# An adaLN block with dilated local attention and a gated feed-forward on one core: softmax in PSUM, its results regrouped by DMA, norm statistics shared with ScalarE, and a new hand-written order

## Chip, cores, metric

One core of one Trainium2 chip. The metric is the device time of one execution in microseconds (us), as the median of several runs. Engines are called PE (TensorE), DVE (VectorE), ACT (ScalarE), POOL (GpSimd) and SP (SyncE, which here only issues DMAs).

## What is computed

```python
mod = (silu(c) @ w_mod).reshape(1, 6, 1, 512)       # sa, ca, ga, sb, cb, gb
h = layernorm(x) * (1 + ca) + sa
x = x + ga * A(h)
h = layernorm(x) * (1 + cb) + sb
x = x + gb * B(h)

# A: 32 heads of 16; a query looks at 8 keys, 2 positions apart, itself the last
q, k, v = heads(x @ wqkv)
idx = pos[:, None] - 2 * arange(8)[None, :]          # masked where idx < 0
attn = softmax(einsum('bhsd,bhswd->bhsw', q, k[idx]) * 16 ** -0.5)
o = einsum('bhsw,bhswd->bhsd', attn, v[idx]);  return o @ wo
# B:
return (gelu(x @ w_gate) * (x @ w_up)) @ w_down
```

2048 positions, model width 512, feed-forward width 1792, inputs and output in bf16.

## The kernel before

The 2048 positions are worked in four groups `sg` of 512 (four blocks `c4` of 128 positions). Each group passes through the same stages. Every stage is a small generator of operations `Op(engine, ...)`; the list `ORDER` at the top of the file names, one after the other, the generator whose next operation is issued. So the order of the instructions on every engine is written out by hand, stages of different groups are interleaved in it, and nothing reorders them later: an instruction that waits holds up all that stand behind it on its engine. The durations and latencies in the `Op` calls are notes for whoever wrote `ORDER`; they make no instruction. `tc.tile_pool` buffers are reused in turn, so a tile of a pool with n buffers waits for the readers of the tile n before it (`NB` holds the counts: four PSUM banks `mm` for matmul results, two `att`, one pair of banks `lg` for the logits).

The stages of a group, with the lines of the profile:

- LN1 (`norm`, L403): `bn_stats`/`bn_aggr` per block on DVE (L419, L420), `rstd` as a power on POOL (L429), normalised `xn` on DVE (L436). One norm, that of LN1 in group 3, is made by `norm_act` from ACT sums instead (L372, L382). `xn` is then transposed: by PE and identity (L451, L474) for the norms in `BY_PE` and for group 0, by a DMA transpose issued on SP (L457) for the others; ACT applies scale and shift (L489).
- q, k, v (L538, L556): 12 results of four 128x512 matmuls, cast to bf16 by ACT (L570, L572, L576). v is stored to DRAM (L582, `vscr`) and loaded back in four shifted copies, one for each 32 partitions (L591, tile `V4`, one buffer).
- Logits: DVE multiplies q by the 8 shifted k for each of four j (L611, `pq`, 128x4096 bf16), PE adds over partitions with a 0/1 matrix of 32 columns, in four column tiles (L625).
- Softmax over the window (`soft`, L633): maximum from PSUM (L642), difference into an SBUF tile `z` (L648), exponential on ACT in place (L653), sum (L658), reciprocal (L664), product `e` (L669). PE regroups `e` by 64 identity matmuls of 32 columns a group, 16 of them in line at a time (L680), and ACT casts the result to `PT` (L689).
- Values: DVE multiplies `PT` by `V4` (L700, `pv`), PE adds (L714), ACT casts (L725), PE applies `woP` (L735), DVE adds x (L744). `woP` was multiplied by the gate ga beforehand (L354).
- LN2, then the feed-forward: for each of 14 `ft`, g and u (L763, four 128x512 matmuls each), gelu and cast on ACT (L796, L803), product `hh` on DVE (L814; `gl` and `ub` have three buffers each); then y (L775, 14 matmuls for each `c4`; L786 for the last block), x added on DVE (L821, L828), store (L846, L837). `Wd` was multiplied by the gate gb (L349).
- The six vectors of `mod`: four as columns by 16 matmuls of one column each (L289), the two gates as full rows, broadcast over all partitions, by four 128x512 matmuls each (L303) and an ACT cast into `gB` (L308).

Matmuls with four column tiles (L625, L680, L714) run four at a time; below they are called quad blocks. The time of the exp and gelu tables is in rows `ACT_TABLE_LOAD` at L653 and L796; a silu table comes first, at L313.

## Time and profile before

| what | value |
|---|---|
| median of 3 runs | 248.04 us (247.26 to 250.15) |
| the profiled execution: its own time | 247.37 us |
| its span, first to last instruction | 245.5 us, so 1.9 us lie outside |
| busy: PE, DVE, ACT, POOL | 235.3, 180.0, 144.0, 16.6 us |
| granted TensorE clock | 1.000 |
| DMA traffic | 27.3 MB |

Columns of the page's groups: line, engine, operation, output<-inputs, shapes, count, then busy time and mean duration of one, then the idle time of the engine before them and what ended it. A matmul's duration counts its way through the array, so back-to-back matmuls overlap; the chain of waits, which gives each piece of work only the time until the next began, shows their real pitch.

### The profile page before, as it was taken

The page shows a single profiled execution, that of the slowest core. Times are in us where ns is not written, and L with a number is a line of the kernel's source. Part 1 is how long each engine was busy: PE and PEld are TensorE (multiplying, and loading weights), DVE is VectorE, ACT ScalarE, POOL GpSimd, SP SyncE. Part 2 cuts the span into 40 slices and gives each one's busy share as a digit, 9 for nine tenths or more (in the row PEclk, how much of TensorE's full clock was granted, in tenths as well). Part 3 has the DMA queues.
Part 4 walks back from the last instruction along what each step waited for, and adds up shares of the span by engine and source line. Part 5 has one row for each costly group of instructions (what it writes and reads, how often), then busy time and mean ns, then how long its engine had stood idle before and what let it go on. Part 6 is the DMA issues. An engine that isn't in the chain of part 4 may idle for free.

```text
span 245.5 us, 3731 instructions
## 1 busy us (share of the span) xinstructions
PE 235.3 (96%) x1431; PEld 110.9 (45%) x1445; DVE 180.0 (73%) x253; ACT 144.0 (59%) x252; POOL 16.6 (7%) x37
## 2 busy tenths in 40 slices
PE   7899678999999999999999999999999999999994
PEld 2655345544453444444444444444444444444444
DVE  4789899989999899898989898677824922222222
ACT  2379698883688576325765835268654424666400
POOL 3450011000400000010000001000000100000000
PEclk9999999999999999999999999999999999999999
DMA  6998699959916009209300592400000061000011
GB/s 168 379 382 269 124 201 250 415 189 217 202 46 208 0 7 211 45 16 201 108 1 3 105 223 44 128 23 0 3 0 0 0 131 64 1 0 3 0 43 43
DMA packets 29289, 27.32 MB, mean 111 GB/s; under 512 B 7256, under 2 KB 28120, under 8 KB 29272
## 3 DMA queue, kind: packets, MB, share of 16 engines
q1 hardware_dynamic: 28976, 26.83, 42.3%
q10 hardware_dynamic: 296, 0.26, 0.4%
q8 instruction: 11, 0.18, 0.3%
q14 instruction: 6, 0.05, 0.1%
HBM read 21.32 MB, written 4.19 MB: 104 GB/s over the span
## 4 chain that ended last, share of the span: by engine, by line
PE 79%; DVE 13%; DMA 4%; POOL 1%; issue 1%; POOLq 0%
PE u_ps L763 19%; PE g_ps L763 19%; PE y_ps L775 18%; PE qkv_ps L556 8%; PE x_ps L735 6%; DMA x<-in_A_x_dram 4%; DVE pq L611 4%; PE o_ps L714 3%; PE LTp L625 2%; DVE st L419 2%; DVE ssum L658 1%; POOL rstd L429 1%; PE y_ps L786 1%; DVE e L669 1%; DVE mx L642 1%; DVE z L648 1%
## 5 line engine op out<-in xcount | busy, mean ns | idle before, releaser
L763 PE MATMUL u_ps<-h,Wu 128*128 128x512 bf16 x224 | 57.5, 379 | 0.0
L763 PE MATMUL g_ps<-h,Wg 128*128 128x512 bf16 x224 | 57.5, 379 | 0.0
L796 ACT ACTIVATE gl<-g_ps 128x512 bf16<-128x512 f32 x56 | 33.6, 601 | 24.9 <-PE g_ps L763 20.6
L775 PE MATMUL y_ps<-Wd,hht 128*128 128x512 bf16 x203 | 45.9, 379 | 0.4
L803 ACT CAST ub<-u_ps 128x512 bf16<-128x512 f32 x56 | 33.0, 589 | 18.2 <-PE u_ps L763 18.1
L814 DVE TENSOR_TENSOR hht<-gl,ub 128x512 bf16<-128x512 bf16 x56 | 22.3, 419 | 29.1 <-ACT ub L803 29.0
L556 PE MATMUL qkv_ps<-hT,wqkv 128*128 128x512 bf16 x184 | 42.2, 380 | 0.0
L700 DVE TENSOR_TENSOR pv<-PT,V 128x4096 bf16<-128x4096 bf16 x16 | 35.8, 2286 | 2.1 <-ACT PT L689 2.1
L611 DVE TENSOR_TENSOR pq<-qT,kT 128x4096 bf16<-128x4096 bf16 x16 | 36.0, 2283 | 0.9 <-PE o_ps L714 0.7
L763 PEld LDWEIGHTS <-Wu 128*128 128x128 bf16 x224 | 21.4, 98 | 27.6 <-issue 2.5
L763 PEld LDWEIGHTS <-Wg 128*128 128x128 bf16 x224 | 21.6, 98 | 26.8 <-issue 1.3
L775 PEld LDWEIGHTS <-hht 128*128 128x128 bf16 x210 | 20.5, 98 | 25.0 <-issue 0.4
L556 PEld LDWEIGHTS <-wqkv 128*128 128x128 bf16 x184 | 20.2, 114 | 19.0 <-issue 2.3
L429 POOL TENSOR_TENSOR rstd<-rstd,neghalf 128x4 f32<-128x4 f32 (+1 forms) x8 | 11.7, 1462 | 174.0 <-DVE rstd L425 174.0
L821 DVE TENSOR_TENSOR ot<-y_ps,x 128x512 bf16<-128x512 f32 x15 | 10.3, 688 | 17.1 <-PE y_ps L775 13.6
L419 DVE BATCH_NORM_STATS2 st<-x 128x6 f32<-128x512 bf16 x28 | 18.9, 675 | 3.0 <-DMA x<-in_A_x_dram 2.9
L489 ACT ACTIVATE h<-h,modT,scl 128x512 bf16<-128x512 bf16 x12 | 8.8, 802 | 15.9 <-DMA h<-xn 15.9
L735 PE MATMUL x_ps<-woP,oT 128*128 128x512 bf16 x60 | 14.9, 379 | 0.2
L570 ACT CAST qT<-qkv_ps 128x512 bf16<-128x512 f32 x16 | 9.5, 601 | 6.5 <-PE qkv_ps L556 5.6
L744 DVE TENSOR_TENSOR x<-x_ps,x 128x512 bf16<-128x512 f32 x16 | 10.7, 684 | 2.7 <-PE x_ps L735 2.7
L572 ACT CAST kT<-qkv_ps 128x512 bf16<-128x512 f32 x16 | 9.5, 602 | 2.8 <-PE qkv_ps L556 2.8
L436 DVE TENSOR_SCALAR xn<-x,mv,rstd 128x512 bf16<-128x512 bf16 x28 | 9.8, 407 | 1.6 <-POOL rstd L429 1.6
(76 smaller groups left out, 175.8 us busy)
## 6 DMA issues: line engine op xcount, KB each, us to landing
V<-vscr SPq DMA_DIRECT2D x12, 520.0 KB, 9.2
wm<-in_w_mod_dram SPq DMA_DIRECT2D x6, 512.0 KB, 7.5
vscr<-vT SPq DMA_DIRECT2D x4, 512.0 KB, 3.8
out_dram<-ot SPq DMA_DIRECT2D x15, 128.0 KB, 1.7
Wg<-in_B_w_gate_dram SPq DMA_DIRECT2D x1, 1792.0 KB
Wu<-in_B_w_up_dram SPq DMA_DIRECT2D x1, 1792.0 KB, 12.8
wqkv<-in_A_wqkv_dram SPq DMA_DIRECT2D x3, 512.0 KB, 8.1
x<-in_A_x_dram SPq DMA_DIRECT2D x3, 512.0 KB, 8.0
```

The costliest lines, as they stand in the source:

```text
L419: nc.vector.bn_stats(out=st_k["st"][:, c4, :], in_=src()[:, c4, :])
L429: nc.gpsimd.tensor_tensor(out=st_k["rstd"][:, a:b], in0=st_k["rstd"][:, a:b], in1=neghalf[:, a:b], op=ALU.pow)
L556: nc.tensor.matmul(ps[:], lhsT=wqkv[blk][:, dt, j::4], rhs=B["hT", sg][:, :, dt, :], start=(dt == 0), stop=(dt == DT - 1))
L611: nc.vector.tensor_tensor(out=pq[:], in0=_ap(B["qT", sg][:, j, :], [[0, W], [1, SG]]), in1=_ap(kT[:, j, sg * SG + 2:sg * SG + 2 + SG], [[2 ...
L700: nc.vector.tensor_tensor(out=t[:], in0=_ap(B["PT", sg][:, 0, :], [[SG, 2], [0, 4], [1, SG]]), in1=_ap(v[:, 0, j, :], [[8, 2], [4 * (SG + ...
L735: nc.tensor.matmul(ps[:], lhsT=B["oT", sg][:, j, c4 * P:(c4 + 1) * P], rhs=woP[:, j, :], start=(j == 0), stop=(j == 3))
L744: nc.vector.tensor_tensor(out=x[:, c4, :], in0=B["x1ps", sg, c4][:], in1=x[:, c4, :], op=ALU.add)
L763: nc.tensor.matmul(ps[:], lhsT=Wt[:, dt, ft * P:(ft + 1) * P], rhs=B["h2T", sg][:, :, dt, :], start=(dt == 0), stop=(dt == DT - 1))
L775: nc.tensor.matmul(ps[:], lhsT=B["hh", sg, ft][:, c4 * P:(c4 + 1) * P], rhs=B["Wd", ft // 4][:, ft % 4, :], start=(ft == 0), stop=(ft == F ...
L796: nc.scalar.activation(out=gl[:], in_=B["g", sg, ft][:], func=ACT.Gelu_apprx_tanh)
L803: nc.scalar.copy(out=ub[:], in_=B["u", sg, ft][:])
L814: nc.vector.tensor_tensor(out=hh[:], in0=B["gl", sg, ft][:], in1=B["ub", sg, ft][:], op=ALU.mult)
```

## The change

- Softmax in place: the tile `z` is gone; the difference, the exponential and its sum work on the logits' PSUM tile `LTp`.
- Groups 1, 2 and 3 (`PT_DMA`): `e` is stored to DRAM and loaded back regrouped by four DMAs on SP, instead of 16 matmuls and two casts. Group 0 keeps PE.
- The gates: 16 matmuls of 32 columns by 128 in four column tiles give four rows of 128 values; ACT casts them, one DMA writes them to DRAM, another loads them broadcast into `gB`.
- Norm statistics: ACT makes them for 13 of the 32 blocks (before: 4), DVE for 19. `LN1.3` leaves `BY_PE`: its transpose is a DMA.
- The exp table is loaded ahead of the first softmax, by an exponential of four unused values.
- Head: x block 0 and 1 come by ACT's queue, 2 and 3 as one DMA by SP's; warm-up has 20 matmuls for 22; the load `wm4` stands behind `woP`; all `wm` share the two `h2` buffers. `prod` has 4 buffers for 3, `stat` 4 for 2. Logits and values use one j at a time in all groups.
- A new `ORDER` (and new notes of durations).

```diff
+PT_DMA = (1, 2, 3)
-          "wm": 1, ...  "prod": 3, "lt": 1, ...
+          ... "prod": 4, ...
+    gscr = {b: dram.tile([D], BF16, name=f"gscr{b}") for b in (2, 5)}
+    escr = {g: dram.tile([P, W, P], BF16, name=f"escr{g}") for g in PT_DMA}
...
-        def f():                                          # row(b, dst)
-            ps = T("mm", [P, D], F32, "mb_ps")
-            for kt in range(4):
-                nc.tensor.matmul(ps[:], lhsT=scB[:, kt, :], rhs=B["wm", b][:, kt, :], ...)
-        def g():
-            nc.scalar.copy(out=dst[:], in_=B["mb", b][:])
+    def gload(k):
+        def f0():
+            nc.sync.dma_start(out=gscr[b].rearrange("(c p) -> c p", p=P), in_=gR[0:P:H, k, :])
+        def f1():
+            nc.sync.dma_start(out=gB[:], in_=bass.AP(gscr[b].tensor, gscr[b].offset, [[0, P], [1, D]]))
+    def mods_g(k):
+            ps = T("mm", [P, P], F32, "gR_ps")
+            for kt in range(4):
+                for ch in range(4):
+                    nc.tensor.matmul(ps[H * ch:H * ch + H, :], lhsT=scB[:, kt, :],
+                                     rhs=B["wm", b][:, kt, ch * P:(ch + 1) * P], ..., tile_position=(0, H * ch))
+            nc.scalar.copy(out=gR[:, k, :], in_=B["mp", b][:])
...
+        yield Op("ACT", 0.15, lambda: nc.scalar.activation(out=junk[:], in_=neghalf[:], func=ACT.Exp), ...)
...
-    BY_ACT = ("LN1.3", )
+    ACT_CH = {"LN1.1": (3, 4), "LN1.2": (2, 4), "LN1.3": (0, 4), "LN2.0": (0, 2), "LN2.1": (0, 4)}
...
-    BY_PE = ("LN1.1", "LN1.2", "LN1.3", "LN2.0")
+    BY_PE = ("LN1.1", "LN1.2", "LN2.0")
...
-    GL = [[1, 1, 1, 1]] + [[2, 2]] * (NSG - 1)            # GV the same
+    GL = [[1, 1, 1, 1]] * NSG
...
-            B["z", sg] = T("lt", [P, W, P], F32, "z")
+            B["z", sg] = B["LT", sg]
...
+        if sg in PT_DMA:
+            return
+    def pt_dma(sg):
+        def f():
+            nc.sync.dma_start(out=escr[sg][:], in_=B["e", sg][:])
+        for a in range(4):
+            def f(a=a):
+                src = bass.AP(escr[sg].tensor, escr[sg].offset + a * P,
+                              [[W * P, H], [4 * P, 2], [H * W * P, CPS], [1, P]])
+                nc.sync.dma_start(out=B["PT", sg][H * (3 - a):H * (3 - a) + H, :, :]
+                                  .rearrange("p t (g s) -> p t g s", s=P), in_=src)
```

In the new `ORDER`, the work between the q, k, v of group 0 and the feed-forward stands so on DVE (counts behind the products; LN stands for the statistics and `rstd` of a norm, xn for its normalised blocks): LN1.1, xn1.1, pq.0 x4, LN1.2, mask, maximum and difference of group 0, xn1.2, pq.1 x1, sum, reciprocal, e.0, xn1.3, pq.1 x2, pv.0 x4, woP, pq.1 x1, x1.0, ..., e.1, pq.2 x4 with four hh, pv.1 x4. On PE the quad blocks of neighbouring j stand together in several places: 32 matmuls in a row for the logits of group 2 (with the gate gb's 16 behind them) and of group 3, and the last logits of group 1's third j next to the first values of group 0.

On SP: ..., vscr of group 0, its first two `V4` loads, the gate ga's store, the third `V4` load, vscr of group 1, the fourth `V4` load, the DMA transpose of LN1.3, the load of `gB`, `Wg`, `Wu`, vscr of group 2, group 1's `V4` loads, the store and four loads of group 1's softmax, `wm5`, ... For group 2 the five softmax DMAs stand behind the first two output stores; for group 3 the store stands before, and its loads behind, the last of group 3's four `V4` loads.

## The prediction

> **What bounds the kernel now.** I read the page first (busy times, the chain), then PE's timeline of the first 40 us, the chain in order of time, and the groups by shape.

> ```profile
> PE 235.3 (96%) x1431; PEld 110.9 (45%) x1445; DVE 180.0 (73%) x253; ACT 144.0 (59%) x252; POOL 16.6 (7%) x37
> ...
> PE 79%; DVE 13%; DMA 4%; POOL 1%; issue 1%; POOLq 0%
> ```

> PE bounds it; DVE's 13% must lie somewhere. PE's timeline (start, length, instructions; in brackets the wait before) shows where:

> ```profile
> 10.84 1.91 PE L538 MATMUL qkv_ps<-hT,wqkv 128*128 128x256 bf16 x16
> ...
> 25.05 0.61 PE L625 MATMUL LTp<-pq,Mph 128*32 128x512 bf16 x8 [0.56 <-DVE pq L611]
> 27.25 0.62 PE L625 MATMUL LTp<-pq,Mph 128*32 128x512 bf16 x8 [1.59 <-DVE pq L611]
> 27.80 5.37 PE L556 MATMUL qkv_ps<-hT,wqkv 128*128 128x512 bf16 x24
> 33.72 0.54 PE L289 MATMUL modT_ps<-scT,wm 128*128 128x1 bf16 x16 [0.55 <-ACT vT L576]
> 34.20 1.89 PE L556 MATMUL qkv_ps<-hT,wqkv 128*128 128x512 bf16 x8
> 37.46 0.62 PE L680 MATMUL PTp<-e,ident 128*32 128x256 bf16 x16 [1.37 <-DVE e L669]
> ```

> From 24 to 39 us PE waits for group 0's logits and softmax: 0.56 + 1.59 + 0.55 + 1.37 = 4.1 us. Later I find one wait, 0.44 us at 78.9, again for e (L669). Otherwise PE runs without a gap until 242.4; behind it lie 3.1 us of last addition and store. So the end moves by what PE no longer does, and by what it no longer waits. The chain in order of time (start, us until the next, what) prices PE's pieces:

> ```profile
> 125.15 0.55 PE PTp L680 x16
> 125.70 0.86 PE LTp L625 x16
> 126.56 0.97 PE u_ps L763 x4
> 127.53 0.86 PE g_ps L763 x4
> ...
> 131.85 0.98 PE o_ps L714 x16
> ```

> Four 128x512 matmuls take 0.86. A block of 16 quad matmuls takes 0.98 entering from full columns and 0.86 behind another quad block, and the first full group after it 0.97: 0.86 of work and 0.22 for the two switches. Eight take 0.43 of work (0.55 with the entry), and a group of 16 PTp also 0.43.

> **PE's work after the head** (against the profiled span).
> - PTp of groups 1 to 3 is gone: 3 x 0.43 = -1.3. ACT loses six casts of 0.5.
> - LN1.3's transposes (16 at L451, 0.89 in the chain): -0.9.
> - Gate gb: four 128x512 (0.86) become 16 quads of 128 columns, four in line: by the pitch of 0.86 / 4 for 512 columns, 4 x 0.054 = 0.2, behind a quad block without a switch: -0.6. (ga lies in the head, where PE waits anyway before; -0.4 there.)
> - Switches: behind group 0's PTp there are 17 separate quad blocks before and 11 after, although single j are used everywhere, because the new order puts them side by side: 6 x 0.22 = -1.3.

> Sum -4.1, and -0.4 for the wait at 78.9.

> **The head.** DVE starts the chain when x of group 1 lands (11.56 before; the same 2.6 MB come first, so I take 11.3). Three blocks of statistics at 0.82 (one is ACT's) end at 13.8; POOL 1.4 from DVE's add to DVE's xn (106.05 to 107.45 in DVE's timeline): 15.25; four xn 1.3: 16.6; four products at 2.22 end at 25.4, where before they end at 27.2. There POOL's rstd took 3.17 us at 15.21 because a product ran beside it; now DVE waits for POOL and that does not occur, since only short or PSUM-fed work follows the power each time. PE's second logits block thus begins at 25.4 and 12 q, k, v results of group 1 follow (10.4), with LN1.2's transposes (0.9) in between: 37.9. The eight logits matmuls of group 1's first j end at 38.4; e is due at 25.4 + LN1.2's two blocks 1.8 + mask 0.3 + 1.26 + 1.14 + xn 1.3 + pq 2.2 + sum + 0.98 + 1.14 = 35.5 + sum.

> ```profile
> L658 DVE TENSOR_REDUCE ssum<-z 128x128 f32<-128x1024 f32 x4 | 7.6, 1910 | 0.0
> ...
> L642 DVE TENSOR_REDUCE mx<-LTp 128x128 f32<-128x1024 f32 x4 | 4.9, 1222 | 0.9 <-PE LTp L625 0.9
> ```

> These groups by shape (busy us, mean ns, idle) show one reduction of one shape: 1.91 from SBUF, 1.22 from PSUM. Reading PSUM now, the sum costs 1.22 to 1.91; I take 1.25, its new source's row. e is ready at 36.8 (37.4 at worst), before PE needs it at 38.4. PTp ends at 39.0, 0.9 later than before (38.1), but with four more results of group 1 (3.5), LN1.2's transposes (0.9) and the first logits block (0.5) behind it: a lead of 4.0 us. The start of q, k, v, at 10.84 before, may come 0.4 earlier (DVE's wait of 0.38 for x's last block, which now travels in SP's first DMA); that is counted in the 4.0.

> [...]

> Nothing else in the head is free by itself. ACT's statistics of group 1 (0.63 + 0.12 + 0.72) stand before its first cast and wait for x: 11.3 to 12.8; then scB (a quarter of L359's elements, 0.62 for all: 0.3) and the casts at 0.49. The first q is cast at 13.6 to 13.7, and PE needs its bank at 13.9; if x lands 1 us later, PE loses 0.8. The exp table (1.28) fills ACT's idle 1.86 before scl (L297); it takes 1.28 off ACT's path to e.0, which other DVE work covers now. wm4 waits for the ga matmuls (20.3) and lands about 24.5, under the wait for logits. The third `V4` load is behind ga's store, the fourth behind group 1's v (35.2), landing about 41.3 (5.5 as its shortest row); group 0's values start at 43 (36.8 + xn 1.3 + two products 4.4 = 42.5 and slack). LN1.3's DMA transpose is issued at 38.3 to 38.9 and lands 4.2 later; ACT comes to its four scalings at 44.3. Behind it `Wg` and `Wu` are issued at 41.5 to 43 instead of 37 to 39 and need 12.8: 56, against a first g at 68.

> **Group by group.** I followed the engines' order with these pitches. PE: values of group 0 at 47.9 and 52.3 (waits 0.3), x1 at 53.8 to 58.0 (0.3), LN2.0 transposes at 64.1, g0 at 68.4, y of group 0 at 100.8 (before 105.9, then with 16 logits matmuls of group 2 still to do, 1.1), y of group 1 at 144.8. Waits that I find, for a bank, a `gl` buffer or oT: 0.3 + 0.3 + 0.3 + 0.1 + 0.2 + 0.1 = 1.3 us. ACT's 12 us more of statistics (9 blocks of 0.63 + 0.72) fall beside x1 and the waiting of ACT for PE (20.6 and 18.1 in the waits).

> The DMA route of the softmax is the unmeasured part. The DMA rows (count, KB, us from issue to landing):

> ```profile
> V<-vscr SPq DMA_DIRECT2D x12, 520.0 KB, 9.2
> ...
> vscr<-vT SPq DMA_DIRECT2D x4, 512.0 KB, 3.8
> out_dram<-ot SPq DMA_DIRECT2D x15, 128.0 KB, 1.7
> ```

> The 256 KB store lies between the last two: 2.4. Then four issues at 0.6 and the last load's landing. No row has 64 KB in pieces of 256 bytes; low 1.7, as the 128 KB store, high 9.2, as the `V4` loads. I take 2.3, since `V4`'s rows carry eight times the bytes and queue behind each other. From e to PT: 0.1 + 2.4 + 0.1 + 1.8 + 2.3 = 6.7 us, bounds 6.1 and 13.6 (PE and ACT before: e ends at 78.8, values start at 80.4, 1.6). Covered by: group 1, four products and four hh, 10.2; group 2, one product, two ot, maximum, difference and two hh with their wait for g and u, 7.7; group 3, `hh`, x, statistics, xn, 8.3. PE's next quad block then has 2, 1.5 and 2.1 us of slack. Nothing to pay at 6.7.

> **Sum.** -4.0 - 4.1 - 0.4 + 1.3 = -7.2: span 238.3, run 240.2 against 247.37. The median lies 0.67 above the profiled run, so 240.9; I say 241.0. Own range 239 to 243: without any of the 1.3, 239.6, and 0.5 below that if x lands early; with 2 us of waits that I overlooked, 243.

> **Rivals.**
> 1. Half the gain: the head's lead is lost. If x of group 1 or its casts come 1.5 us late, PE loses most of that, and LN1.3's transpose or the fourth `V4` load, late by 2.5 (the spread of the `V4` landings is 5.5 to 13.4), holds ACT and DVE: -7.2 + 1.2 + 2.0 = -3.2, 244.8. For it: 0.2 us between cast and bank; against: these loads have no neighbours.
> 2. No change to speak of: hh in feed-forward 0 starves. DVE does nine products and `Wd`'s scaling (7 x 0.6) there, with `gl` three deep; each product displaced by a late one costs 2.2, three of them 6.6: 247.4 on the median's scale. For it: ACT's waits for hh, 4.1 us before. Against: DVE has 10 us less to do overall (9 blocks of 0.82, four sums of 0.66).
> 3. Slower: the round trip of the softmax. Each us beyond 6.7 is covered by 5.5, 2.5 and 3.7 us in groups 1, 2, 3, and then stops DVE's values, hence x1 and LN2, and PE. At the high bound, 13.6, it costs 1.4 + 4.4 + 3.2 = 9.0: 250.0. It decides from about 13.0, where it eats 7.2. For it: the `V4` rows, whose tail is 13.4; against: eight times the bytes. [...]
> 4. The change does not do what it says, the sum staying at 1.91 from PSUM and the quad blocks switching between every j (10 more switches, 2.2): -4.5, 243.5.

> **Numbers.** Forecast 0.64; rival 1 0.12, 2 0.06, 3 0.10, 4 0.08. A measurement of this kernel tells about 1% (2.5 us) from no change. Faster by over 1% (below 245.6): forecast, rival 4 and most of 1, 0.82; same: rival 2 and the rest of 1, 0.08; slower 0.10. The range goes to 246.0, with rivals 2 and 3 beyond, and down to 239.0.

> **What would show it.** Right: PTp of group 0 near 39 with group 1's q, k, v behind it and no wait over 1.5 us before; sum rows at 1.25; no PE wait in the 50 us of feed-forward 0 above 0.5; PT landing under 7 us after e; PE's end near 235.2. Wrong: DVE pv waiting for a DMA (rival 3); ACT waiting for hht by more than 6 us (2); DVE or ACT waiting for x, V or hT by DMA before 50 us (1); 0.97 behind every eight quads (4).

## The result, and the profile after

The changed kernel takes 241.27 us (median of 4 runs, 240.55 to 242.38) against 248.59 for the kernel before beside it: a ratio of 0.971 (95% interval 0.964 to 0.978), 7.3 us less. Run once more in the experiments it gave 0.972 (0.966 to 0.977); there the medians are 5.6 us apart (246.65 and 241.04), since the kernel before, 248.59 in the first set, has medians of 246.65 to 247.26 in the four later ones. Forecast were 241.0 us and a span of 238.3; the profiled execution took 241.38 us, with a span of 239.6 (before 247.37 and 245.5). So the median fits better than the working: of 7.2 us predicted on the profiled span, 5.9 came. Medians and ratios leave disturbed executions out, among them the profiled ones of the repeat (405.95 us) and of the longer softmax route (249.63 us), whose profile serves only to show which waits occur.

The page of the changed kernel, busy times and the chain's shares:

```profile
PE 232.5 (97%) x1392; PEld 109.6 (46%) x1403; DVE 170.0 (71%) x238; ACT 150.7 (63%) x287; POOL 12.4 (5%) x37
...
PE 90%; DMA 4%; ACT 4%; issue 0%; ACTq 0%; DVE 0%
```

DVE's 13% of the chain are gone, but 4% of ACT are new. DMA had 4% before, for x; of its 4% now half is the load of `wm`. PE's timeline of the head shows where:

```profile
10.87 1.91 PE L543 MATMUL qkv_ps<-hT,wqkv 128*128 128x256 bf16 x16
...
22.97 0.55 PE L292 MATMUL modT_ps<-scT,wm 128*128 128x1 bf16 x16 [0.20 <-ACT kT L577]
23.45 1.05 PE L630 MATMUL LTp<-pq,Mph 128*32 128x512 bf16 x16
26.04 0.55 PE L292 MATMUL modT_ps<-scT,wm 128*128 128x1 bf16 x16 [1.55 <-DMA wm<-in_w_mod_dram]
26.52 1.55 PE L630 MATMUL LTp<-pq,Mph 128*32 128x512 bf16 x16
28.00 8.22 PE L561 MATMUL qkv_ps<-hT,wqkv 128*128 128x512 bf16 x32
...
40.50 0.62 PE L630 MATMUL LTp<-pq,Mph 128*32 128x512 bf16 x8
40.95 0.64 PE L688 MATMUL PTp<-e,ident 128*32 128x256 bf16 x16
```

The waits for products, a cast and e, 4.1 us before, are gone. In their place stands one of 1.55 us for the load of `wm4`. Behind it work is longer than its kind: the second 16 logits matmuls take 1.55 where the first took 1.05. The windows (stretch; length, busy time of PE, PEld, DVE, ACT, POOL; granted clock; DMA share; GB/s) say why:

```profile
26.00:27.00 1.00, 0.96 (x25) 0.70 (x29) 0.94 (x3) 1.00 (x6) 0.00 (x0) 0.96 0.11 35
27.00:28.00 1.00, 1.00 (x12) 0.16 (x5) 0.42 (x3) 0.94 (x5) 0.45 (x1) 0.50 0.09 16
...
30.00:31.00 1.00, 1.00 (x5) 0.48 (x4) 1.00 (x2) 1.00 (x2) 0.00 (x0) 0.83 1.14 253
```

The granted clock is 0.50 for some 3.4 us, from the end of the 27th us to the 31st, and 1.00 everywhere else; that takes half of it from PE, some 1.7 us (an estimate; the experiments measure it). In the profile of before it was 1.00 throughout.

One mark divides the rest: the start of the first feed-forward matmul. It is 73.8 us before and 70.4 after (predicted 68.4); from there to the end of the span it is 171.7 before and 169.2 after. The head gave 3.4 us, the work behind it 2.5.

Three views answer to those shown of before. The chain in order of time:

```profile
78.37 1.84 PE LTp L630 x32
80.21 0.22 PE gR_ps L345 x16
80.44 0.97 PE u_ps L786 x4
```

Thirty-two logits matmuls and the gate's sixteen stand behind one entry and one exit, as priced (0.2 for the gate). The groups by shape, and the DMA rows of 60 to 160 us (count, KB, us to landing):

```profile
L647 DVE TENSOR_REDUCE mx<-LTp 128x128 f32<-128x1024 f32 x4 | 4.9, 1221 | 0.1
L663 DVE TENSOR_REDUCE ssum<-LTp 128x128 f32<-128x1024 f32 x4 | 4.8, 1212 | 0.0
```

```profile
escr<-e SPq DMA_DIRECT2D x3, 256.0 KB, 2.5
PT<-escr SPq DMA_DIRECT2D x12, 64.0 KB, 2.4
```

The sum takes 1.21 us from PSUM (1.91 from SBUF before). The 64 KB loads in pieces of 256 bytes land in 2.4 us.

### The profile page after: what moved, and what is told of

It reads as the page before. It is cut to its first block, busy times and chain, and to the rows that moved or that the text cites. A ratio compares the mean times of both kernels' runs of the same rounds, so it can differ in the third digit from the quotient of the medians.

```text
span 239.6 us, 3678 instructions
## 1 busy us (share of the span) xinstructions
PE 232.5 (97%) x1392; PEld 109.6 (46%) x1403; DVE 170.0 (71%) x238; ACT 150.7 (63%) x287; POOL 12.4 (5%) x37
## 4 chain that ended last, share of the span: by engine, by line
PE 90%; DMA 4%; ACT 4%; issue 0%; ACTq 0%; DVE 0%
PE g_ps L786 20%; PE u_ps L786 20%; PE y_ps L798 19%; PE qkv_ps L561 14%; PE x_ps L758 6%; PE o_ps L737 3%; PE LTp L630 3%; DMA wm<-in_w_mod_dram 2%; DMA c<-in_c_dram 2%; PE y_ps L809 1%; ACT hT L494 1%; ACT gl L395 1%; PE warm_ps L210 1%; PE qkv_ps L543 1%; ACT vT L581 1%; PE modT_ps L292 1%
## 5 line engine op out<-in xcount | busy, mean ns | idle before, releaser
L798 PEld LDWEIGHTS <-hht 128*128 128x128 bf16 x210 | 20.6, 98 | 24.8
L561 PEld LDWEIGHTS <-wqkv 128*128 128x128 bf16 x184 | 20.6, 114 | 20.3 <-issue 3.5
L443 POOL TENSOR_TENSOR rstd<-rstd,neghalf 128x4 f32<-128x4 f32 (+1 forms) x9 | 8.6, 956 | 160.2 <-DVE rstd L437 89.6
L406 DVE BATCH_NORM_STATS2 st<-x 128x6 f32<-128x512 bf16 x19 | 12.8, 675 | 2.9 <-DMA x<-in_A_x_dram 2.9
L748 ACT CAST oT<-o_ps 128x512 bf16<-128x512 f32 x16 | 8.8, 592 | 5.5 <-PE o_ps L737 5.4
L581 ACT CAST vT<-qkv_ps 128x512 bf16<-128x512 f32 x16 | 9.2, 605 | 1.2 <-PE qkv_ps L561 1.2
## 6 DMA issues: line engine op xcount, KB each, us to landing
wm<-in_w_mod_dram SPq DMA_DIRECT2D x6, 512.0 KB, 5.8
vscr<-vT SPq DMA_DIRECT2D x4, 512.0 KB, 3.7
out_dram<-ot SPq DMA_DIRECT2D x15, 128.0 KB, 1.7
wqkv<-in_A_wqkv_dram SPq DMA_DIRECT2D x3, 512.0 KB, 9.3
x<-in_A_x_dram SPq DMA_DIRECT2D x3, 512.0 KB, 8.6
```

The costliest lines, as they stand in the source:

```text
L406: nc.vector.bn_stats(out=st[:], in_=src()[:, c4, :])
L561: nc.tensor.matmul(ps[:], lhsT=wqkv[blk][:, dt, j::4], rhs=B["hT", sg][:, :, dt, :], start=(dt == 0), stop=(dt == DT - 1))
L581: nc.scalar.copy(out=B["vT", sg][:, j, :], in_=ps[:])
L798: nc.tensor.matmul(ps[:], lhsT=B["hh", sg, ft][:, c4 * P:(c4 + 1) * P], rhs=B["Wd", ft // 4][:, ft % 4, :], start=(ft == 0), stop=(ft == F ...
```

## The experiments

**The head.** The theory: the wait for `wm4` and the clock behind it ate what the head was to give. `wm4` stands behind the four `woP` loads in SP's queue, and takes an `h2` buffer that gate a's matmuls must free first (issued at 20.93). The rival: casts and statistics on ACT, over which the chain runs from 32 to 41 us, hold the head. The kernel again, to see how steady its clock is:

> The kernel after once more, unchanged, beside the other three on the same chip, to have a second profiled execution of it and a tighter ratio. Expected: 0.97 times the kernel before. If a pause of PE of about 1.5 us is near the point from which the granted clock falls, the load of wm4 lands between 25.0 and 26.3 us (as it did in the kernels that share it), PE waits for it 1.0 to 1.8 us, and the clock behind it is 0.50 in some executions and 1.00 in others; if the fall has another cause, it is at 27 us again.

241.0 us, ratio 0.972. Its profile can't be read for the landing of `wm4`, but its executions answer the question on the clock: with those of the first result there are nine, whose median of 241.15 is meant by "after" below. Eight had a mean granted clock of 0.985 to 0.993 and took 240.55 to 242.38; the ninth had 0.999 and took 239.38. So the fall comes in most executions, not in all, and costs about 1.8 us by the one without it. The kernel before knows it too: of 17 executions beside `a_wm4_wo` below, four had 0.993 (248.95 to 249.43), thirteen 0.998 or more (246.07 to 247.19).

`wm4` in another buffer, same place in the queue:

```diff
-                B["wm", b] = T("h2", ...)
+                B["wm", b] = T("q" if b == 4 else "h2", ...)
-            yield Op("SP", 0.6, ldwm(4), take=[SL["h2"]], ...)
+            yield Op("SP", 0.6, ldwm(4), take=[SL["q"]], ...)
```

> The kernel after, with the load of wm4 taking its buffer from the pool of the later q tiles instead of the h2 tiles, so that it no longer waits until gate a's matmuls have read one. In the kernel after, this load is issued at 20.93 and PE waits 1.55 us for it at 26.04; behind that wait the granted clock is 0.50 for about 3.3 us. Theory (the wait sets back the head, and the pause behind it costs the clock): the wait goes, 1.2 to 1.6 us, and if the halved clock goes with it another 1.0 to 1.7; the time falls by 1.2 to 2.7 us against the kernel after, to 238.6 to 240.1. Rival (the stretch from 28 to 41 us is bound by the ACT engine's casts and statistics, which end no earlier): the time falls by at most 0.5 us. Between them: the wait goes and the clock still falls, because the little transposes of the gates are what lets it fall: 1.0 to 1.5 us.

241.2 us, ratio 0.975 (0.972 to 0.978): nothing gained. The load was issued at 17.16 in place of 20.93 and landed at 25.92 all the same, behind the `woP` loads (three of them landed at 23.7 to 24.7); PE waited 1.82 and the clock fell to 0.50. The buffer alone was not the cause.

The wait filled, with the load where it was:

```diff
+            if b == 4:
+                wp = T("mm", [P, SG], F32, "fill_ps")
+                for _ in range(7):
+                    nc.tensor.matmul(wp[:], lhsT=gB[:, 0:P], rhs=gB[:], start=True, stop=True)
```

> The kernel after, with seven more 128x512 matmuls of zeros, whose result nobody reads, ahead of the second modulation's matmuls for wm4, so that PE works through the wait at 26.04 instead of standing. Theory (a pause of PE lets the granted clock fall to 0.50): the load lands when it did, so the 1.55 us of wait stay (filled), the clock stays at 0.95 or above from 27 to 31 us, and the time falls by 1.0 to 1.7 us against the kernel after. Rival one (the clock's fall has another cause, say the sparse transposes and modulations around it): the clock still falls and the time is 0 to 0.5 us longer. Rival two (ACT bounds the stretch behind): the clock stays up and the time falls by at most 0.5 us.

239.82 us (238.69 to 240.52), ratio 0.970 (0.967 to 0.973). All six executions had a clock of 1.000; the first feed-forward matmul started at 69.1 (70.4), and 169.2 us followed as before. PE does 1.5 us more of useless work and the kernel is 1.3 us shorter than after by the medians: the clock's fall was the pause's doing, and its price is 1.3 by this run (1.8 by the one execution above). ACT alone does not bound that stretch.

`wm4` ahead in the queue, first too far (ahead of `x3`, `wm2`, `wm3` and `woP`; `x3` behind `wm3`):

```diff
             yield Op("SP", 0.55, ldx(2), ...)
-            yield Op("SP", 0.55, ldx(3), ...)
+            yield Op("SP", 0.6, ldwm(4), take=[SL["q"]], ...)
             ...                                   # wm2, wm3
+            yield Op("SP", 0.55, ldx(3), ...)
             ...                                   # woP, without wm4 behind it
```

> The kernel after, with the load of wm4 put ahead of the loads of wm2, wm3, x3 and wo in SyncE's queue (buffer from the pool of the later q tiles; x3 behind wm3). In the variant that only took the other buffer, the load was issued at 17.16 in place of 20.93 and landed at 25.92 all the same: the DMA engines were 99 per cent busy until 22 us, and the four wo loads ahead of it took 9 us each. Theory (wm4 is late because of what stands ahead of it in the queue): it lands before 21, PE's wait at 24 to 26 us is gone or under 0.3, the clock stays at 1.00, and the time falls by 1.3 to 2.6 us against the kernel after (ratio to before 0.960 to 0.966). Rival (ACT and DVE, not PE, set the head's end; or wm2, wm3 or x3, now one block later, are waited for instead): at most 0.5 us.

242.2 us, ratio 0.978 (0.973 to 0.983): 1.1 longer than after by the medians, against the theory's 1.3 to 2.6 shorter. The chain tells what came in its place:

```profile
13.83 10.37 DMA x<-in_A_x_dram
24.20 0.02 issue
24.22 0.72 ACT gl L384 x2
24.94 0.48 ACT kT L577
25.43 0.02 issue
25.45 2.31 DVE pq L616
```

`x3` was issued late and landed at 24.20. ACT's statistics of it stand in ACT's queue ahead of a cast of k, the last product needs that cast, and PE waited 2.3 us for the product, the clock falling to 0.50 again: the rival's case. `wm4` was in time. Then moved ahead of `woP` alone, where the kernel before has it (and with its buffer from the other pool, as above):

```diff
+            yield Op("SP", 0.6, ldwm(4), take=[SL["q"]], ...)
             for i in range(4):
                 yield Op("SP", 0.45, ld(woP[H * i:H * i + H, :, :], wo_v[i]), ...)
-            yield Op("SP", 0.6, ldwm(4), take=[SL["h2"]], ...)
```

> The kernel after, with the load of wm4 ahead of the four wo loads in SyncE's queue, where the kernel before has it, and its buffer from the pool of the later q tiles; nothing else in the queue moves. Theory (wm4 is late because it stands behind the wo loads; in the variant that put it ahead of x3 too, x3 came late, ACT's statistics of x3 stood before a cast of k, and PE waited 2.3 us for the product instead): wm4 lands at 22 to 24, PE does not wait for it, x3 is where it was, and the clock stays at 1.00; the first feed-forward matmul starts 1.2 to 2.5 us earlier than the 70.4 of the kernel after, and the time is 238.5 to 240.0 (ratio 0.960 to 0.967). Rival (some other operand of that stretch, x2, x3 or the products, then ends 1 us later and PE waits as long): within 0.5 us of the kernel after.

238.25 us (238.12 to 239.09), ratio 0.964 (0.959 to 0.969). Its slowest run is below the fastest of the nine of after, and its clock was 1.000 in all six. This version beats both kernels. Place and buffer were changed together; the place alone was not tried. Its PE timeline:

```profile
22.63 1.05 PE L630 MATMUL LTp<-pq,Mph 128*32 128x512 bf16 x16
24.04 0.55 PE L292 MATMUL modT_ps<-scT,wm 128*128 128x1 bf16 x16 [0.36 <-DMA wm<-in_w_mod_dram]
24.52 1.23 PE L630 MATMUL LTp<-pq,Mph 128*32 128x512 bf16 x16
25.68 7.10 PE L561 MATMUL qkv_ps<-hT,wqkv 128*128 128x512 bf16 x32
...
37.50 0.72 PE L688 MATMUL PTp<-e,ident 128*32 128x256 bf16 x16
```

The eight q, k, v results take 7.10 where they took 8.22, and group 0's turn comes at 37.5, not 40.95. The first feed-forward matmul starts at 67.2, 1.2 earlier than predicted, and again 169.2 us follow. Of the 3.2 us against after, 0.4 come from an earlier start of q, k, v in this profile (10.43 against 10.87).

**The softmax by DMA.** The turns of groups 1 to 3 (16 matmuls a group by the traces, 64 in all four and not in each) given back to PE and ACT, with `ORDER` otherwise kept. Three placings were tried, since `ORDER` was written for the DMA.

```diff
-PT_DMA = (1, 2, 3)
+PT_DMA = ()
 ORDER = [   # a group's five entries of pt_dma out, three of soft in (turn, cast, cast)
```

> The kernel after, with the softmax results of groups 1 to 3 turned by PE transposes with two ACT casts each again, in place of five DMAs each. Theory (PE's queue is the path, each turn costs it about 0.65 us): the time rises by 1.9 us (1.3 to 2.4) against the kernel after. Rival (the DMA round trip of 7 to 8 us from e to the turned tile is what PE's sums with v wait for, and the turn by PE takes 1.6 us): the time stays within 0.5 us or falls.

250.64 us, ratio 1.013 (1.009 to 1.017): 9.5 longer than after. The waits (sum, times, longest):

```profile
ACT PT L696 <- PE PTp L687: 8.1, 3, 4.5
...
PE g_ps L785 <- ACT gl L818: 2.9, 1, 2.9
```

The casts stood in ACT's queue ahead of the GELUs that free PE's banks: ACT stood, then PE, then the clock fell to 0.50, twice for 3.4 us. That tells of the placing.

> The kernel after, with the softmax results of groups 1 to 3 turned by PE and two ACT casts again, and each turn set behind feed-forward matmuls whose results ACT has already queued ahead of its casts. In the first variant of this kind the casts stood in ACT's queue ahead of the GELUs that empty PSUM: ACT waited 4.5 us for the turn and PE 2.9 us for ACT, the clock fell twice, and the time was 9 us longer, which tells of that placing and not of the turn. Theory (a turn costs PE 0.6 to 0.7 us and nothing else): 1.9 us longer than the kernel after (1.3 to 2.5). Rival one (the DMA round trip of 7 to 8 us costs as much as it saves): within 0.5 us. Rival two (ACT's two casts, 1.1 us, delay the GELUs that PE waits for, wherever the turn stands): 3 us longer or more, with PE waits on ACT behind each turn.

246.4 us, ratio 0.996 (0.991 to 1.000): 5.3 longer than after. Group 2's turn now came at 125.7, its values were late, and PE waited 2.2 us for them and 0.7 for x.

> The kernel after, with the softmax results of groups 1 to 3 turned by PE and two ACT casts each, third placing: group 1's turn 2.6 us earlier and group 2's 4.3 us earlier than in the second, each behind two GELUs that ACT has queued ahead of its casts. In the second placing the sum closed as: three turns of 0.7, 2.1; waits of PE for group 1's and group 2's products with v and for x, 2.9; a halved clock behind the longest of them, 1.6. Theory (those waits came from the placing, the turn itself costs 0.7): 1.9 to 2.6 us longer than the kernel after, with no PE wait above 0.5 us after 70 us. Rival (ACT's two casts delay the GELUs wherever the turn stands, or DVE's products come late in any case): 4 us longer or more, with PE waits on ACT or on products.

245.64 us, ratio 0.994 (0.990 to 0.997): 4.5 longer than after. The theory's 1.9 to 2.6 did not come, the rival's 4 did. From the first feed-forward matmul to the end it takes 174.2 us, 5.0 more than after. PE is busy 2.7 longer (235.2 against 232.5); its waits there add up to 2.4. Two of 0.48 are for ACT's cast `ub`, right behind the turns; the largest, 1.22, is for group 2's values. DVE's timeline shows for group 1 how a turn delays them:

```profile
77.51 0.43 DVE L834 TENSOR_TENSOR hht<-gl,ub 128x512 bf16<-128x512 bf16 x1 [2.12 <-ACT ub L823]
...
80.72 6.69 DVE L720 TENSOR_TENSOR pv<-PT,V 128x4096 bf16<-128x4096 bf16 x3
```

`PT` of group 1 was ready at 77.0, as early as by DMA (76.3 in after), but DVE stood 2.12 us for `ub`, which stood behind the two casts; so the values began at 80.7 (79.0 in after). In group 2 they began at 125.6 (121.0). A turn on PE thus costs its PE time and two casts of ACT at a place where PE and DVE wait for ACT. Whether an order written for it could do better was not tried; each of these three was dearer than PE's part alone.

Then the route itself made longer:

```diff
-            nc.sync.dma_start(out=escr[sg][:], in_=B["e", sg][:])
+            nc.sync.dma_start(out=escr0[sg][:], in_=B["e", sg][:])
+            nc.sync.dma_start(out=escr[sg][:], in_=escr0[sg][:])
```

> The kernel after, with one more DRAM-to-DRAM copy of each group's softmax result in the route of groups 1 to 3, which lengthens the way from e to the turned tile, 7 to 8 us, by 2.5 to 3.5. Theory (DVE has other work that covers the longer way, 5.5, 2.5 and 3.7 us beyond 6.7 as the prediction put it, of which 1 has been used): 0 to 0.8 us longer, DVE idle before the first product with v of group 2 only. Rival (the cover is nearly used up at 7 to 8 us, since the first sums with v in PE follow the products closely): 1.5 to 3 us longer, with PE waits for products in groups 2 and 3. Rival two (nothing shows at all: covered by three groups of work): within 0.2 us.

243.75 us, ratio 0.985 (0.979 to 0.992): 2.6 longer by the medians, 4.3 at a clock of 0.999 or more (three executions with a median of 243.7, against the one of after). The theory's 0.8 is exceeded; the first rival's size came, but its reason is only part of it:

```profile
DVE pv L726 <- DMA PT<-escr: 3.8, 2, 2.1
...
PE gR_ps L347 <- DMA wm<-in_w_mod_dram: 2.4, 1, 2.4
```

DVE waited 1.68 us for group 2's tile and 2.08 for group 3's. From e to the values lay 9.8 and 10.4 us, so other work of DVE covers 8.1 and 8.3, as predicted (7.7 and 8.3). The 2.5 and 3.7 beyond 6.7 in the prediction and in the theory hold 1.5 and 2.1 of slack of PE besides. In group 3 PE indeed did not wait for the values; in group 2 it waited 1.2 of the 1.7, so 0.5 was there. The larger part has nothing to do with the cover: `wm5`, behind the four loads in SP's queue, was issued at 79.5 in place of 74.7 (1.6 of that is this execution's later start), and PE waited 2.4 for it.

**The softmax in PSUM.** In the kernel before, for the first group alone:

```diff
-            B["z", sg] = T("lt", [P, W, P], F32, "z")
+            B["z", sg] = B["LT", sg] if sg == 0 else T("lt", [P, W, P], F32, "z")
```

> The kernel before, with the softmax of the first group alone kept in PSUM (its sum, its division and its exp there instead of in an SBUF tile). Theory (in the first group nothing but the softmax is left for PE to do, and the sum of the exps takes 1.22 us from PSUM against 1.91 from SBUF): PE's wait of 1.37 us for e shrinks by about 0.7, and the time falls by 0.5 to 0.9 us against the kernel before. Rival (the wait is set by ACT's other work, or the exp into PSUM is dearer than into SBUF by as much): within 0.2 us.

245.95 us, ratio 0.997 (0.993 to 1.000): 0.8 us by the ratio, 1.3 by the medians; the theory's 0.5 to 0.9 lies in the interval. At a clock of 0.998 or more the medians are 1.4 apart (245.73 and 247.15), so the theory is rather low. In its profile PE's wait for e is 0.7 (1.4). The other way round, `z` back in SBUF in the kernel after, all groups:

```diff
-            B["z", sg] = B["LT", sg]
+            B["z", sg] = T("q", [P, W, P], F32, "z")
```

> The kernel after, with the logits less their maximum written to an SBUF tile again in all four groups, so that the exps and their sum are read from SBUF. Theory (a DVE saving of 0.69 us for each group, from the sum alone, of which only the first group's lies on the path): DVE is busy 2.5 to 2.8 us longer in all, e of the first group comes 0.7 later, and the time rises by 0.3 to 0.9 us against the kernel after. Rival one (DVE is covered by PE in all four groups): within 0.2 us. Rival two (what the first group alone showed in the kernel before, 1.36 us, holds here for the first and, in part, for the others): 1.2 us or more.

241.43 us, ratio 0.975 (0.969 to 0.980): 0.3 us longer by the medians, 0.7 by the ratios, not settled by either interval. The sum takes 1.92 from SBUF again and DVE is busy 172.5 us against 170.0. At an equal clock it is clearer: three executions at 0.993 have a median of 241.9 (the eight of after: 241.2), three at 1.000 one of 240.6 (after: 239.4, one execution). Some 0.7 to 1.2 us, the upper end of the theory or a little above it.

**The fourth norm by PE** again, in the version with `wm4` ahead of `woP`, whose steady clock shows small things:

```diff
-    BY_PE = ("LN1.1", "LN1.2", "LN2.0")
+    BY_PE = ("LN1.1", "LN1.2", "LN1.3", "LN2.0")
 ORDER = [   # two entries for PE, next to group 0's logits and values, for one on SP
```

> The variant with wm4 ahead of the wo loads (238.25 us, no wait above 0.4 us in its head, clock 1.00 in every run), with the transposes of group 3's first norm made by PE again (two blocks of eight between group 0's logits and values blocks) and scaled from PSUM, in place of the DMA transpose. Theory (every piece of work given to PE moves the end by its length): 16 transposes 0.9 and one more switch from quad to full columns 0.2: 0.9 to 1.2 us longer than that variant, ratio to before 0.967 to 0.970. Rival one (the DMA transpose, issued for 3 us and landing 4 to 5 us later, holds ACT, and its removal gives something back): within 0.4 us. Rival two (as with the softmax turns, the second engine that the work needs, here ACT's scaling from PSUM, delays others): 2 us or more.

241.31 us, ratio 0.976 (0.971 to 0.980): 3.1 longer than that version, against 0.9 to 1.2 by the theory; the second rival's 2 or more came. From group 0's turn to the first feed-forward matmul it is 2.8 longer. The two blocks take 1.1 and a switch 0.2; the rest is one wait:

```profile
51.16 0.62 PE L734 MATMUL o_ps<-pv,Msum 128*32 128x512 bf16 x8 [1.54 <-ACT hT L491]
```

The transposes use one of the two `att` banks that the values also need, and ACT frees it only by its scaling. The DMA transpose had not only taken 0.9 us from PE but kept a bank free.

## Why the prediction was right

- **The bound**: PE, as read. Its waits of 4.1 us in the head went, and behind the head no wait of PE is left in after. How much of the 4.1 each change of the head took away was tested for the softmax in PSUM alone; the statistics on ACT, the early exp table and the new order were not varied.
- **PE's work behind the head**: predicted -1.8 behind the first feed-forward matmul (7.2 less the 5.4 of the head, 73.8 to 68.4), measured -2.5. The gate's 0.2, the switches and the reduction are in the rows as priced (behind group 0's turn the rows have 16 separate quad blocks before, not 17, since the logits at 77.38 and the turn at 78.87 stand side by side; after has the 11). The term that was mis-sized is the +1.3 of new waits: at most 0.7 of it lay behind the mark, and none came.
- **The head**: predicted -5.4 to that mark, measured -3.4. The step that failed reads "wm4 waits for the ga matmuls (20.3) and lands about 24.5, under the wait for logits". It landed at 26.0, the logits ahead of it were done at 24.5, and it was costed at nothing. Two prices hang on it: 1.55 us of pause, and the clock's fall. With `wm4` ahead of `woP` the mark comes at 67.2: the lead was there in the order, and 1.2 us more. The holder was named by half: the load did wait for the buffer, but with the buffer free it landed no earlier, because of what stood ahead in the queue. Rival 1 had the place, a lost lead in the head, but not the cause; its sum, -7.2 + 1.2 + 2.0, is -4.0 and not -3.2 (244.0).
- **e and the turn**: e was predicted for 36.8 and PE's need of it at 38.4; e was ready at 39.3 and the turn came at 40.95, because PE's and ACT's work behind the pause was late. With `wm4` ahead of `woP` they came at 36.55 and 37.5.
- **The start of q, k, v**, "0.4 earlier": 10.87 in this profile of after (10.84 before), but 10.26 to 10.77 in nine of its ten variants and 11.34 in the tenth; a variant of the kernel before had 10.60. It scatters by about 1 us, mostly on the early side, and one profile can't tell.
- **The sum over the exps**: 1.25 taken, from the row of the maximum over PSUM; 1.21 measured, against 1.92 for the same reduction from SBUF in `a_z_sbuf`.
- **The DMA route** (rival 3): 6.7 us predicted, 7.6, some 6.9 and some 7.5 measured from e to the tile in groups 1 to 3, mostly because the first load was issued 3.4 and 3.1 us behind the store in groups 1 and 3 (2.1 in group 2), where 2.5 had been taken. It cost nothing, since it stayed inside the cover, which was read rightly: the values began 10.3, 8.0 and 8.2 us behind e (predicted 10.2, 7.7 and 8.3). Only PE's slack behind group 2's values was too large by 1.0, and what stands behind the loads in SP's queue had no term at all. The 64 KB loads land in 2.4 us, where 2.3 had been taken; no run here has the same loads in longer pieces.
- **The signs**: no wait of PE above 0.5 in feed-forward 0 and the sum's rows came as said, and rival 2's sign stayed away (ACT waited 2.7 us for `hht`, 4.1 before). Three signs of being right failed: the turn of group 0 near 39 (40.95), no wait over 1.5 ahead of it (1.55), `PT` under 7 us behind e (7.6 and 7.5).
- **The total**: the span came 1.3 longer than the sum's 238.3, 2.0 too little in the head less 0.7 more behind it. That the median is nearer is luck: 0.8 had been added for the median's place above the profiled run, and here it lies 0.1 below it. At a clock of 0.999 the one execution of after took 239.4, against 246.1 to 247.2 for before at 0.998 or more beside `a_wm4_wo`: 6.7 to 7.8 us, around the predicted 7.2.

## What to carry to other kernels

A load costed at nothing because a wait covers it has to be compared with the time when the consumer's other work ends, and what fixes its landing can be what stands ahead of it in the queue, more than when its buffer comes free (here an issue 3.8 us earlier moved the landing by 0.1). Where PE is the bound, a pause can cost as much again through the clock (here 1.55 us of pause and another 1.3 to 1.8), so look at the granted clock behind each pause; filling the pause with useless matmuls can pay where the load can't be moved (1.3 us in `a_fill`). Work taken off PE also takes off its casts and its banks: in three placings of the softmax turns and in the fourth norm, putting it back cost more than its PE time, in an order that was written without it (at best 4.5 us for 2.7 of PE, and 3.1 for 1.3).

## What the runs showed of the hardware

```profile
122.00:123.00 1.00, 0.00 (x0) 0.00 (x0) 0.00 (x0) 0.99 (x3) 0.00 (x0) 0.74 0.00 0
125.00:126.00 1.00, 1.00 (x4) 0.37 (x3) 1.00 (x1) 0.56 (x1) 0.00 (x0) 0.55 0.08 16
146.00:147.00 1.00, 1.00 (x5) 0.34 (x3) 0.97 (x4) 0.40 (x2) 0.00 (x0) 0.69 0.46 79
149.00:150.00 1.00, 1.00 (x4) 0.35 (x3) 0.00 (x0) 0.26 (x1) 0.07 (x1) 0.60 0.00 0
```

By these shares the clock fell at 122.5, rose at 125.9, fell at 146.4 and rose at 149.8: the falls last 3.4 us, and between them lies six times that. In after the fall lies six times 3.41 us behind the first clock record of the trace (6.45 and 26.93; the rise follows at 30.34), and the two falls of `a_pt_slow` begin 58.0 apart, seventeen times. If each profile is cut into such pieces from its first clock record up to the end of PE's work, the pauses of PE above 0.1 us in a piece, with the half microsecond that 16 matmuls of one column take counted as pause, add up to 1.77 to 2.36 us in all eleven pieces behind which the clock fell, and to 1.60 or less in all others but one (1.79, at the start of `a_ln13_pe`). So the fall goes with a piece in which PE had little to do for about half of the time. A pause that lies across the border of two pieces may go free: the 1.54 us of `a_ln13_pe` divide into 1.2 and 0.3. This is an estimate from thirteen profiles, in which the ends of matmuls are modelled. No experiment moved a pause within the grid, and the second half of the fall of 6.8 us does not fit: the piece before it holds 1.05.
